# Maxima split and turned by one engine and sent straight to the query rows, operands laid out as they are loaded

## The chip, the core and the metric

The kernel runs on one core of a Trainium2 chip. The core has five engines, each with its own queue of instructions: TensorE (PE in the profile) multiplies matrices, VectorE (DVE) reduces and computes element by element, ScalarE (ACT) applies functions, GpSimd (POOL) computes element by element more slowly, and SyncE (SP) asks for transfers between memory (HBM) and on-chip memory. Engines run side by side and wait for each other through semaphores. TensorE writes into eight banks of an accumulation memory (PSUM); a bank may be written again when its reader is done. The metric is the time of one execution on the device in microseconds (us), lower is better, as the median of several runs.

## The reference

The input x is a sequence of 2048 tokens of width 512. The result mixes a 32-head attention (head width 16) and a gated feed-forward layer (inner width 1792), token by token:

```python
x = A_x
g = _sigmoid((x * gate_w).sum(-1, keepdims=True))
a = _A_ref(x, A_wqkv, A_wo)
b = _B_ref(x, B_w_gate, B_w_up, B_w_down)
return g * a + (1 - g) * b
```

```python
scores = jnp.einsum("bhqd,bhkd->bhqk", q, k) * scale
p = _softmax(scores, axis=-1)
o = jnp.einsum("bhqk,bhkd->bhqd", p, v)
...
g = jnp.einsum("bsd,df->bsf", x, w_gate)
u = jnp.einsum("bsd,df->bsf", x, w_up)
h = _sigmoid(g) * u
return jnp.einsum("bsf,fd->bsd", h, w_down)
```

## The kernel before

Everything is float32. For accuracy a product of two operands is made of three: each operand is split into a high part (rounded to a shorter format that TensorE takes) and a low part (the rest), and high x high, high x low and low x high are summed.

**Attention.** Heads go in 16 pairs. For a pair, `QS` and `KS` hold the query and key rows, one head in partitions 0 to 63 and one in 64 to 127. The softmax needs the largest score of each query. It is found first: a pass of matmuls (L282, in `sm_step`) makes scores of 128 queries by 512 keys, and VectorE reduces each to one column (L284). Sixteen such reductions complete a *part*: the maxima of 512 queries of one head, in a tile `stat` of 128 partitions by 4 blocks by 4. `turn_max` then turns a part: VectorE reduces the four columns of each query to one (L296, tile `msq`) and transposes it (L298, tile `mt`), so that queries lie along a row. The maxima, split in high and low, are written into two spare rows of `QS` (rows 48 and 49 of each half), where the second pass of matmuls (L577, in `st_part`), which takes 64 rows where the first took 48, subtracts them. ScalarE takes the exponential (L579), and TensorE multiplies with the values (L710, in `values`).

The way from `mt` to the rows of `QS` has two halves, and `turn_max` gives back a function for each. `send` splits on GpSimd (L98, L99, tile `mhl`) and writes 128 rows to memory at `m_d` (L302). `back` reads two rows from there into `QS` (L308), one transfer for the high and one for the low parts.

**Order.** The main loop has 256 periods (`for k in range(NPER)`), and each is written out by hand: `STEADY` holds two lists of words, and for each word the next matmul of a stream is put on TensorE's queue: `m0`, `m1` scores for maxima, `t0`, `t1` scores for the exponential, `d0`, `d1` half a matmul of other work (64 rows), so that two streams fill the two halves of TensorE. After each list come the 32 matmuls of the values. Seven banks go round between the streams by a table (`REUSE`). The `d` work is, first, query and key projections of later heads (`Sum`, L148), then the feed-forward layer (`Side`, L168), which is computed from mixtures of blocks of x and of the weights.

Work that is not on TensorE's list stands in a queue of closures, `later`. One is taken at the word `work`, three or four after each list, so these closures set the order of GpSimd and of the transfers that follow them on SyncE. After a list, `turn_max` is called for each full part; its `send` is put at the front of `later`, and its `back` is called two periods on. A part falls due every second period, from the two halves in turn. All transfers but two stand on SyncE's queue in the order in which the program was written, and each waits until the eighth transfer before it has landed.

**Mixtures.** `mixing` makes sums and differences of blocks of x on GpSimd, 16 pieces for each of two column pairs: `load` fetches up to four half tiles (L326), GpSimd adds and splits (L331, L347, L335), and the result goes to memory (L336), from where `mixed` reads it back (L356). `mixtures` does the same for weights: `raw` fetches tiles `r0` to `r5` (L376) as one or two half tiles each. `turn` puts a token on GpSimd's queue (L176) that a later matmul on TensorE waits for; it keeps the two halves from writing one bank at once.

Of the kernel before, what the change touches and what calls it, by code (L numbers as in the profile page):

```python
# [12 lines left out]
F32 = mybir.dt.float32  # L13
# [27 lines left out]
UPPER = FIRST + 4  # L41
EARLY = NPER - TAIL - 4
LOW, UP = 0, 1


@with_exitstack
def gated_mix(ctx, tc, x, xc, wqk, wv, wo, w_gu, w_down, gate_w, out):
    nc = tc.nc
    pe, act, dve, pool, sp = nc.tensor, nc.scalar, nc.vector, nc.gpsimd, nc.sync

# [25 lines left out]
    m_d = dram.tile([NPAIR, NC, 2, P, 2, 32], F32, name="m_d")  # L76

    warm = keep.tile([P, 1], F32, name="warm")
    dve.memset(warm, 0.0)
# [166 lines left out]
                    yield sp.dma_start((QS, KS)[t][p % 2][r:r + DH, cols].bitcast(F32), src[a, rows, cols])  # L246
# [22 lines left out]
    def sm_step(j):  # L269

        p, s = divmod(j, 32)
        qt, kh = divmod(s, 2)
        qs, ks = QS[p % 2], KS[p % 2]

        def one(b, i):
            part = (p, qt // 4, b)
            if part not in stat:
                stat[part] = keep.tile([P, 4, 4], F32, name=f"stat{p}_{qt // 4}_{b}", tag="stat", bufs=8)
                count[part] = 0
            r, g = 64 * b, 2 * kh + i  # L280
            t = bankm()
            pe.matmul(t, qs[r:r + KM, qt * P:(qt + 1) * P], ks[r:r + KM, g * 512:(g + 1) * 512],  # L282
                      start=True, stop=True)
            dve.tensor_reduce(stat[part][:, qt % 4, g:g + 1], t, axis=AX.X, op=ALU.max)  # L284
            count[part] += 1
            if count[part] == 16:
                full.append(part)
        return one
# [3 lines left out]
    def turn_max():  # L292
        part = full.pop(0)
        p, i, b = part
        m = square()
        dve.tensor_reduce(m[:, :4], stat.pop(part), axis=AX.X, op=ALU.max)  # L296
        mt = keep.tile([P, 32], F32, name=f"mt{p}_{i}_{b}", tag="mt", bufs=2)
        dve.transpose(mt, m)  # L298
        def send():
            hl = keep.tile([P, 2, 32], F32R, name=f"mhl{p}_{i}_{b}", tag="mhl", bufs=2)  # L300
            split(hl[:, 0, :], hl[:, 1, :], mt, pool, pool)
            sp.dma_start(m_d[p, i, b], hl.bitcast(F32))  # L302

        def back():
            rows = m_d[p, i, b].rearrange("(g t) a j -> a t g j", g=4)
            for a in range(2):
                r = 64 * b + 3 * DH + a
                sp.dma_start(QS[p % 2][r:r + 1, i * 512:(i + 1) * 512].bitcast(F32).rearrange(  # L308
                    "o (t g j) -> o t g j", g=4, j=32), rows[a, :4].unsqueeze(0))
        return send, back  # L310

    SIDES = (slice(0, 64), slice(64, 128))
    MIX = (((0, 0), "+", (1, 1)), ((0, 0), None, None)), (((0, 1), "-", (1, 1)), ((1, 0), "-", (0, 0))), (
        ((0, 0), "+", (0, 1)), ((1, 0), "+", (1, 1))), (((1, 1), None, None), ((1, 1), None, None))

    def mixing(pair):

        def load(j, b):
            e = keep.tile([P, 2, 512], F32R, name=f"xm{pair}_{j}_{b}", tag="ev", bufs=2)
            f = e.bitcast(F32)  # L320
            for g in (UP, LOW):
                first, sign, second = MIX[j][1 - g]
                for i, half in enumerate((first, second)):
                    if half:
                        r, c = half
                        sp.dma_start(f[SIDES[g], i, :], xc[2 * pair + c, 2 * r + b // 2, SIDES[b % 2], :])  # L326
# [12 lines left out]
        loaded = []  # L339
        later.append(lambda: loaded.append(load(*pieces[0])))  # L340
        for n, (j, b) in enumerate(pieces):
            yield
            signs = [MIX[j][1 - g][1] for g in (LOW, UP)]
            for rows, sign in zip([slice(0, P)] if signs[0] == signs[1] else SIDES, signs):
                if sign:
                    later.append(lambda n=n, r=rows, op=ALU.add if sign == "+" else ALU.subtract: add(loaded[n], r, op))
            later.append(lambda n=n: pool.tensor_copy(loaded[n][:, 1, :], loaded[n].bitcast(F32)[:, 0, :]))  # L347
# [18 lines left out]
    def mixtures():  # L366
        for cp in range(2):
            for fp in range(NF // 2):
                for a in range(2):
                    name = f"{cp}_{fp}_{a}"  # L370

                    def raw(n, *parts):
                        t = keep.tile([P, 512], F32, name=f"r{n}_{name}", tag="wr", bufs=4)
                        for (f, r), sides in parts:
                            for g in sides:
                                sp.dma_start(t[SIDES[g], :], w_gu[a, 2 * fp + f, r])  # L376
                        return t
# [9 lines left out]
                    x0 = raw(0, ((0, 0), [UP]), ((1, 0), [LOW]))  # L387
                    x1 = raw(1, ((1, 1), [UP, LOW]))
                    yield
                    w = ready(0, x0, x1, ALU.add)  # L390
                    r = raw(2, ((0, 0), [UP]), ((1, 1), [LOW]))
                    yield w
                    w = ready(1, r)
                    y = raw(3, ((1, 0), [UP]), ((0, 1), [LOW]))
# [3 lines left out]
                    z0 = raw(4, ((0, 0), [side]))  # L398
                    z1 = raw(5, ((0, 1), [side]))
# [184 lines left out]
    for t in range(2, NS, 2):  # L584
        two = [Sum(bankv(), tokens(t + a)) for a in range(2)]
        for g in (LOW, UP):
            first_max()
            for m in range(3 * KT):
                two[0].half(g)
                two[1].half(1 - g)  # L590
                if m == 5 or m == 8 and (g == LOW or t == 2):
                    first_max()
                if t == NS - 2 and (g, m) in ((LOW, 8), (UP, 2), (UP, 5), (UP, 8)):
                    next(ahead)
                while full:
                    for go in turn_max():
# [184 lines left out]
    outs, backs = [], []  # L781
    backlog = []
    for k in range(NPER):
        n = 2 * k
# [12 lines left out]
        else:  # L797
            group["t1"] = chain(st_part(k, 1), st_part(k + 1, 1))
        emit(STEADY[k % 2] if k < NPER - TAIL else LAST[k - NPER], **group)
        for go in backs:  # L800
            go()
# [138 lines left out]

def by_blocks(w):
    w = np.asarray(w)
    return w.reshape(2, 2, 2, 64, NF, P).transpose(4, 0, 3, 1, 2, 5).reshape(NF, 2, 64, 512)


# [20 lines left out]
```

## Time and profile before

| what | value |
|---|---|
| median of 3 runs | 1700.06 us (1697.31 to 1703.04) |
| the profiled execution | 1701.52 us, its span 1699.7 us, mean granted clock 0.996 |
| share of TensorE, VectorE, ScalarE, GpSimd that is busy | 99%, 85%, 79%, 60% |
| `xm<-in_xc_dram`, SyncE | 104 transfers, 128 KB each |
| `r<-in_w_gu_dram`, SyncE | 280 transfers, 128 KB each |
| `m_d<-mhl`, SyncE | 128 transfers, 32 KB each |
| `qs<-m_d`, SyncE | 256 transfers, 2 KB each |
| `pv_d<-sum`, SyncE | 64 transfers, 128 KB each |

A row of the profile names line, engine, operation and tiles (written<-read), with durations in us, or in ns where it says mean. An entry in brackets tells how long the engine stood idle before the row, and what ended it. "SPq" is SyncE's queue. A busy share is an average: what a change is worth is read at the places where TensorE stands still.

### The profile page before, as it was taken

Reading aid. Unit: us, or ns where it says so; the run is one execution under the profiler, and the core shown is the slowest. Engines: PE = TensorE matmul, PEld = TensorE weight load, DVE = VectorE, ACT = ScalarE, POOL = GpSimd, SP = SyncE. Lnnn points to the kernel's source line nnn. Section 1 sums busy time; section 2 is a strip of 40 time slices with the busy share of each in tenths; the row PEclk is TensorE's granted clock in tenths of the full one; section 3 lists DMA queues with packets and bytes.
Section 4 is the critical chain, followed back from the end, with each engine's and each line's share of the span. In section 5 each row is a group of like instructions: output and inputs, shape, how many; then the busy total and the mean of one; then the engine's idle time right before and its main releaser. Section 6 shows DMA issues by size and latency. Waiting matters only on the chain.

```text
span 1699.7 us, 43409 instructions
## 1 busy us (share of the span) xinstructions
PE 1684.2 (99%) x16552; PEld 1155.1 (68%) x16552; DVE 1441.1 (85%) x2450; ACT 1336.3 (79%) x2668; POOL 1026.5 (60%) x1193
## 2 busy tenths in 40 slices
PE   9999998999999999999999999999999999999999
PEld 7866665666666666666666566666666666578887
DVE  6899997999999999999998799999999999567543
ACT  4188886888888888888888799999999988973321
POOL 1146664358888787777664777777776765352110
PEclk9999999999999999999999999999999999999999
DMA  9625677364445454443347342424243423276752
GB/s 258 112 86 164 181 209 194 121 159 134 129 135 142 131 132 144 125 116 89 89 139 186 110 110 80 124 87 112 93 113 92 108 83 101 69 255 227 246 195 72
DMA packets 148944, 231.70 MB, mean 136 GB/s; under 512 B 40384, under 2 KB 57024, under 8 KB 145728
## 3 DMA queue, kind: packets, MB, share of 16 engines
q1 hardware_dynamic: 148448, 228.41, 47.4%
q8 instruction: 130, 2.13, 0.6%
q14 instruction: 78, 0.64, 0.1%
q10 hardware_dynamic: 288, 0.52, 0.1%
HBM read 148.90 MB, written 79.95 MB: 135 GB/s over the span
## 4 chain that ended last, share of the span: by engine, by line
PE 81%; DMA 1%; SPq 0%; ACT 0%; issue 0%; DVE 0%; POOL 0%; ACTq 0%
PE dn L168 23%; PE sm L710 18%; PE sm L282 8%; PE st L282 7%; PE sm L914 7%; PE st L710 6%; PE sm L577 4%; PE st L135 3%; PE st L577 2%; PE dn L914 2%; PE dn L148 2%; DMA m_d<-mhl 1%; DMA xm<-xm_d 0%; DMA xm<-in_xc_dram 0%; ACT p L579 0%; SPq L376 0%
## 5 line engine op out<-in xcount | busy, mean ns | idle before, releaser
L284 DVE TENSOR_REDUCE stat<-sm 128x1 f32<-128x512 f32 x1124 | 728.2, 682 | 66.4 <-PE st L577 26.8
L579 ACT ACTIVATE p<-sm 128x512 f32<-128x512 f32 x1217 | 686.8, 630 | 18.0 <-PE sm L577 15.7
L284 DVE TENSOR_REDUCE stat<-st 128x1 f32<-128x512 f32 x924 | 607.0, 683 | 62.7 <-PE st L282 24.6
L579 ACT ACTIVATE p<-st 128x512 f32<-128x512 f32 x831 | 499.4, 634 | 2.4 <-PE st L282 0.7
L168 PE MATMUL dn<-xm,mh 64*128 64x512 f32 x1568 | 486.4, 390 | 5.7 <-DMA xm<-xm_d 5.7
L577 PE MATMUL sm<-qs,ks 64*128 64x512 f32 x1217 | 447.0, 405 | 0.3 <-ACT p L579 0.2
L282 PE MATMUL sm<-ks,qs 48*128 48x512 f32 x1124 | 420.6, 422 | 0.3 <-ACT p L579 0.3
L282 PE MATMUL st<-ks,qs 48*128 48x512 f32 x924 | 369.1, 427 | 0.0
L710 PE MATMUL sm<-p,v 128*17 128x256 f32 x6080 | 366.2, 381 | 0.1
L577 PE MATMUL st<-qs,ks 64*128 64x512 f32 x831 | 325.6, 409 | 0.0
L168 PEld LDWEIGHTS dn<-xm,mh 64*128 64x128 f32 x1568 | 289.6, 185 | 35.2 <-DMA xm<-xm_d 7.3
L168 PE MATMUL dn<-xm,ml 64*128 64x512 f32 x784 | 304.8, 389 | 0.0
L728 POOL TENSOR_TENSOR sum<-sum,part 128x256 f32<-128x256 f32 x192 | 141.6, 737 | 256.5 <-ACT part L715 237.3
L710 PEld LDWEIGHTS sm<-p,v 128*17 128x17 f32 x6080 | 160.5, 97 | 170.6 <-ACT p L579 58.8
L282 PEld LDWEIGHTS sm<-ks,qs 48*128 48x128 f32 x1124 | 200.5, 185 | 85.9 <-DVE stat L284 57.6
L577 PEld LDWEIGHTS sm<-qs,ks 64*128 64x128 f32 x1217 | 219.3, 186 | 18.9 <-ACT p L579 3.3
L282 PEld LDWEIGHTS st<-ks,qs 48*128 48x128 f32 x924 | 167.7, 185 | 83.3 <-DVE stat L284 66.9
L410 POOL TENSOR_TENSOR m<-m,m 128x512 f32<-128x512 f32 x140 | 178.2, 1289 | 2.8 <-ACT m L512 2.5
L577 PEld LDWEIGHTS st<-qs,ks 64*128 64x128 f32 x831 | 152.7, 186 | 12.3 <-ACT p L579 1.5
L168 PEld LDWEIGHTS dn<-xm,ml 64*128 64x128 f32 x784 | 144.7, 185 | 11.9
L121 POOL TENSOR_TENSOR ml<-r,mh 128x512 fp32r<-128x512 f32 x112 | 144.0, 1286 | 7.7
L512 ACT ACTIVATE m<-dn 128x512 f32<-128x512 f32 x196 | 132.8, 677 | 0.0
(225 smaller groups left out, 2180.4 us busy)
## 6 DMA issues: line engine op xcount, KB each, us to landing
r<-in_w_gu_dram SPq DMA_DIRECT2D x280, 128.0 KB
gul<-gu_d SPq DMA_DIRECT2D x56, 512.0 KB
gu_d<-m SPq DMA_DIRECT2D x84, 256.0 KB
xm_d<-xm SPq DMA_DIRECT2D x32, 512.0 KB
xm<-xm_d SPq DMA_DIRECT2D x32, 512.0 KB
xm<-in_xc_dram SPq DMA_DIRECT2D x104, 128.0 KB
qs<-q_d SPq DMA_DIRECT2D x90, 128.0 KB
ks<-k_d SPq DMA_DIRECT2D x90, 128.0 KB
```

The lines of the kernel that those rows point to most:

```text
L121: pool.tensor_tensor(l, src, h.bitcast(F32), ALU.subtract)
L135: pe.matmul(o, a, b, start=(i == 0), stop=(i == len(ops) - 1))
L168: pe.matmul(self.o, a, b, start=(self.n == 0), stop=(self.n == len(self.ops) - 1))
L282: pe.matmul(t, qs[r:r + KM, qt * P:(qt + 1) * P], ks[r:r + KM, g * 512:(g + 1) * 512], start=True, stop=True)
L284: dve.tensor_reduce(stat[part][:, qt % 4, g:g + 1], t, axis=AX.X, op=ALU.max)
L410: pool.tensor_tensor(o, x, y, op)
L512: leave = lambda e, o: act.activation(e, o, AF.Copy)
L577: pe.matmul(o, ks[r:r + KR, (kt + a) * P:(kt + a + 1) * P], qs[r:r + KR, c * 512:(c + 1) * 512], start=True, stop=True)
L579: act.activation(pt[:, a, :], o, AF.Exp, scale=DH ** -0.5)
L710: pe.matmul(o[r:r + VW, :], v[:, 4 * k % 16 + a, h * VW:(h + 1) * VW], pts[b][:, a, 256 * i:256 * i + 256], start=(a == 0), stop=(a == 3))
L728: pool.tensor_tensor(s, s, e, ALU.add)
L914: pe.matmul(down[t], a, b, start=(f == 0 and m == 0), stop=(f == NF - 2 and m == 5))
```

## The change

Three things are changed.

1. `turn_max` splits before it transposes. VectorE reduces into `mx`, casts that to the high parts (L300 of the changed kernel), subtracts for the low parts (L301), with high and low of each block side by side in `msq`, and transposes four overlapping blocks of 32 columns at once (L305), so that high and low parts come out in neighbouring partitions. `send` is then four transfers from `mt` straight to the rows of `QS`, for four groups of 32 partitions. `back`, `m_d`, `mhl` and GpSimd's two instructions are gone. `stat` has 6 buffers in place of 8, `msq` one in place of two.
2. The host gives the blocks of x (`xmix`) and of the gate and up weights (`w_gu`) in the arrangement in which they are loaded, so that each piece of `xm` and each of `r0` to `r5` is one transfer.
3. The list of changes that came with it names token sums asked for by SyncE; in the diff no line of theirs is changed, but for what moves in line numbers.

```diff
-    square = ring(keep, 2, [P, 32], "msq")
-    for _ in range(2):
-        pool.memset(square(), 0.0)
+    square = turns([(keep.tile([P, 4], F32, name=f"mx{i}"), keep.tile([P, 40], F32R, name=f"msq{i}")) for i in range(1)])
+    for _ in range(1):
+        pool.memset(square()[1].bitcast(F32), 0.0)
...
-        m = square()
-        dve.tensor_reduce(m[:, :4], stat.pop(part), axis=AX.X, op=ALU.max)
-        mt = keep.tile([P, 32], F32, name=f"mt{p}_{i}_{b}", tag="mt", bufs=2)
-        dve.transpose(mt, m)
+        m, hl = square()
+        dve.tensor_reduce(m, stat.pop(part), axis=AX.X, op=ALU.max)
+        two = hl[:, :8].rearrange("p (t c) -> p t c", c=2)
+        dve.tensor_copy(two[:, :, 0], m)
+        dve.tensor_tensor(two[:, :, 1], m, two[:, :, 0].bitcast(F32), ALU.subtract)
+        f = hl.bitcast(F32)
+        blocks = bass.AP(f.tensor, f.offset, [f.ap[0], (2, 4), (1, 32)])
+        mt = keep.tile([P, 4, 32], F32, name=f"mt{p}_{i}_{b}", tag="mt", bufs=2)
+        dve.transpose(mt, blocks)
+
         def send():
-            hl = keep.tile([P, 2, 32], F32R, name=f"mhl{p}_{i}_{b}", tag="mhl", bufs=2)
-            split(hl[:, 0, :], hl[:, 1, :], mt, pool, pool)
-            sp.dma_start(m_d[p, i, b], hl.bitcast(F32))
-
-        def back():
-            rows = m_d[p, i, b].rearrange("(g t) a j -> a t g j", g=4)
-            for a in range(2):
-                r = 64 * b + 3 * DH + a
-                sp.dma_start(QS[p % 2][r:r + 1, i * 512:(i + 1) * 512].bitcast(F32).rearrange(
-                    "o (t g j) -> o t g j", g=4, j=32), rows[a, :4].unsqueeze(0))
-        return send, back
+            r = 64 * b + 3 * DH
+            rows = QS[p % 2][r:r + 2, i * 512:(i + 1) * 512].bitcast(F32).rearrange("a (t g j) -> a g t j", g=4, j=32)
+            for g in range(4):
+                sp.dma_start(rows[:, g], mt[32 * g:32 * g + 2])
+        return send
...
-            for g in (UP, LOW):
-                first, sign, second = MIX[j][1 - g]
-                for i, half in enumerate((first, second)):
-                    if half:
-                        r, c = half
-                        sp.dma_start(f[SIDES[g], i, :], xc[2 * pair + c, 2 * r + b // 2, SIDES[b % 2], :])
+            n = max(1 + (second is not None) for _, _, second in MIX[j])
+            sp.dma_start(f[:, :n, :], xmix[pair, j, b, :, :n, :])
...
-                    def raw(n, *parts):
+                    def raw(n, rows=slice(0, P)):
                         t = keep.tile([P, 512], F32, name=f"r{n}_{name}", tag="wr", bufs=4)
-                        for (f, r), sides in parts:
-                            for g in sides:
-                                sp.dma_start(t[SIDES[g], :], w_gu[a, 2 * fp + f, r])
+                        sp.dma_start(t[rows, :], w_gu[a, fp, n, rows, :])
                         return t
...
-        for go in backs:
-            go()
-        backs, outs, turned = outs, [], []
+        turned = []
         while full:
-            send, back = turn_max()
-            turned.append(send)
-            outs.append(back)
+            turned.append(turn_max())
```

How this moves instructions is shown at two places, with the buffers' numbers and the semaphores that each instruction waits for (DMAHW0 to DMAHW7 tell of transfers). First VectorE, where it turns a part of pair 8 in the main loop, before:

```order
L284 TENSOR_REDUCE stat8_0_0_10624<-sm0_69 128x1 [waits PE_49]
L296 TENSOR_REDUCE msq0_112<-stat8_0_1_10458 128x4 [waits DVE_49]
L298 STREAM_TRANSPOSE mt8_0_1_10743<-msq0_112 128x32 [waits DVE_49,Pool_49]
L284 TENSOR_REDUCE stat8_1_1_10772<-sm3_72 128x1 [waits PE_49]
L284 TENSOR_REDUCE stat8_0_0_10624<-st0_65 128x1 [waits PE_49]
```

and the same place of the changed kernel, whose lines are numbered otherwise (L286 is the reduction of scores):

```order
L286 TENSOR_REDUCE stat8_0_0_10508<-sm0_69 128x1 [waits PE_49]
L298 TENSOR_REDUCE mx0_111<-stat8_0_1_10342 128x4 [waits DVE_49]
L300 CAST msq0_112<-mx0_111 128x4 [waits DVE_49]
L301 TENSOR_TENSOR msq0_112<-mx0_111,msq0_112 128x4 [waits DVE_49]
L305 STREAM_TRANSPOSE mt8_0_1_10627<-msq0_112 128x128 [waits DMAHW2_49,DMAHW1_49,DMAHW7_49,DMAHW0_49,DVE_49]
L286 TENSOR_REDUCE stat8_1_1_10654<-sm3_72 128x1 [waits PE_49]
```

Two instructions come in between, each waits for the one ahead of it, and the transposition waits for the four transfers that read the tile's buffer two turns before, where it waited for GpSimd. Second SyncE, where the part `1_1` (pair 1, queries 512 to 1023) of one head is sent, before:

```order
L730 DMA pv_d_77<-sum0_3_1981 128x256 [waits DMAHW7_49,Pool_49]
L302 DMA m_d_79<-mhl1_1_0_2275 128x64 [waits DMAHW0_49,Pool_49]
L336 DMA xm_d_75<-xm0_1_2_2193 256x1x512 [waits DMAHW1_49,Pool_49]
L326 DMA xm0_1_3_2282<-in_xc_dram 64x512 [waits DMAHW2_49]
L326 DMA xm0_1_3_2282<-in_xc_dram 64x512 [waits DMAHW3_49]
L326 DMA xm0_1_3_2282<-in_xc_dram 64x512 [waits DMAHW4_49]
L326 DMA xm0_1_3_2282<-in_xc_dram 64x512 [waits DMAHW5_49]
L246 DMA qs0_103<-q_d_73 16x2048 [waits DMAHW6_49]
L246 DMA ks0_104<-k_d_74 16x2048 [waits DMAHW7_49]
L308 DMA qs1_105<-m_d_79 1x16x32 [waits DMAHW0_49]
L308 DMA qs1_105<-m_d_79 1x16x32 [waits DMAHW1_49]
```

and of the changed kernel:

```order
L722 DMA pv_d_77<-sum0_3_1967 128x256 [waits DMAHW1_49,Pool_49]
L311 DMA qs1_104<-mt1_1_0_2174 2x4x32 [waits DMAHW2_49,DVE_49]
L311 DMA qs1_104<-mt1_1_0_2174 2x4x32 [waits DMAHW3_49]
L311 DMA qs1_104<-mt1_1_0_2174 2x4x32 [waits DMAHW4_49]
L311 DMA qs1_104<-mt1_1_0_2174 2x4x32 [waits DMAHW5_49]
L331 DMA xm_d_75<-xm0_1_2_2179 256x1x512 [waits DMAHW6_49,Pool_49]
L321 DMA xm0_1_3_2265<-in_xmix_dram 128x1024 [waits DMAHW7_49]
L248 DMA qs0_102<-q_d_73 16x2048 [waits DMAHW0_49]
L248 DMA ks0_103<-k_d_74 16x2048 [waits DMAHW1_49]
```

The maxima go from `mt` to `QS` at the place where they went to memory; they wait for VectorE instead of GpSimd, and the two transfers that waited for the first to land are gone from the queue. The load of `xm` is one transfer. On TensorE and ScalarE the order is unchanged, and on GpSimd the two instructions of each split are left out.

More of the change, by code (lines that the diff above doesn't have):

```diff
@@ L43, with gated_mix @@
 LOW, UP = 0, 1
+MIX = ((((0, 0), "+", (1, 1)), ((0, 0), None, None)), (((0, 1), "-", (1, 1)), ((1, 0), "-", (0, 0))),
+       (((0, 0), "+", (0, 1)), ((1, 0), "+", (1, 1))), (((1, 1), None, None), ((1, 1), None, None)))
+BLOCKS = (((0, 0), (1, 0)), ((1, 1), (1, 1)), ((0, 0), (1, 1)), ((1, 0), (0, 1)), ((0, 0), (0, 0)), ((0, 1), (0, 1)))
 @with_exitstack
-def gated_mix(ctx, tc, x, xc, wqk, wv, wo, w_gu, w_down, gate_w, out):
+def gated_mix(ctx, tc, x, xc, xmix, wqk, wv, wo, w_gu, w_down, gate_w, out):
     nc = tc.nc
@@ L75, in gated_mix @@
     rec_d = dram.tile([P, 512], F32, name="rec_d")
-    m_d = dram.tile([NPAIR, NC, 2, P, 2, 32], F32, name="m_d")
     warm = keep.tile([P, 1], F32, name="warm")
@@ L277, in one @@
             if part not in stat:
-                stat[part] = keep.tile([P, 4, 4], F32, name=f"stat{p}_{qt // 4}_{b}", tag="stat", bufs=8)
+                stat[part] = keep.tile([P, 4, 4], F32, name=f"stat{p}_{qt // 4}_{b}", tag="stat", bufs=6)
                 count[part] = 0
@@ L397, in mixtures @@
                     side = LOW if a else UP
-                    z0 = raw(4, ((0, 0), [side]))
-                    z1 = raw(5, ((0, 1), [side]))
+                    z0 = raw(4, SIDES[side])
+                    z1 = raw(5, SIDES[side])
                     yield w
@@ L595, in gated_mix @@
                 while full:
-                    for go in turn_max():
-                        go()
+                    turn_max()()
             if g == LOW:
@@ L780, in gated_mix @@
     bank = bankm = place
-    outs, backs = [], []
     backlog = []
@@ L942, in by_blocks, with by_mixtures, rows @@
     w = np.asarray(w)
-    return w.reshape(2, 2, 2, 64, NF, P).transpose(4, 0, 3, 1, 2, 5).reshape(NF, 2, 64, 512)
+    w = w.reshape(2, 2, 2, 64, NF, P).transpose(4, 0, 3, 1, 2, 5).reshape(NF // 2, 2, 2, 64, 512)
+    return np.stack([np.concatenate([w[:, f, r] for f, r in (low, up)], axis=1) for up, low in BLOCKS], axis=1)
+def by_mixtures(xc):
+    def rows(pair, j, b, g, i):
+        half = MIX[j][1 - g][2 * i]
+        r, c = half or MIX[j][1 - g][0]
+        return xc[2 * pair + c, 2 * r + b // 2, 64 * (b % 2):64 * (b % 2) + 64]
+    return np.array([[[[[rows(pair, j, b, g, i) for i in range(2)] for g in (LOW, UP)] for b in range(4)]
+                      for j in range(4)] for pair in range(2)]).transpose(0, 1, 2, 3, 5, 4, 6).reshape(2, 4, 4, P, 2, 512)
 def kernel(A_x, A_wqkv, A_wo, B_x, B_w_gate, B_w_up, B_w_down, gate_w):
+    xc = np.asarray(A_x)[0].T.reshape(KT, P, NC, 512).transpose(2, 0, 1, 3)
     host = {
         "x": np.asarray(A_x)[0],
-        "xc": np.asarray(A_x)[0].T.reshape(KT, P, NC, 512).transpose(2, 0, 1, 3),
+        "xc": xc,
+        "xmix": by_mixtures(xc),
         "wqk": by_tiles(A_wqkv)[:8],
```

11 lines of the change are left out of this document (4 added, 7 removed).

## The prediction

> **What bounds the kernel now.** I read the page first: engine shares, then the chain of work that ended last.
>
> ```profile
> span 1699.7 us, 43409 instructions
> PE 1684.2 (99%) x16552; PEld 1155.1 (68%) x16552; DVE 1441.1 (85%) x2450; ACT 1336.3 (79%) x2668; POOL 1026.5 (60%) x1193
> PE 81%; DMA 1%; SPq 0%; ACT 0%; issue 0%; DVE 0%; POOL 0%; ACTq 0%
> ```
>
> TensorE sets the end almost alone. Nothing in the change takes a matmul away, so time can only come from where TensorE stands still, and be lost where something new makes it stand still. The next view is the busy time of each engine in stretches of 25 us; these are the columns PE, PEld, DVE, ACT, POOL, then the granted clock, the DMA share and GB/s. I looked for stretches where PE is under 25.00.
>
> ```profile
> 275.00:300.00 25.00, 20.68 (x190) 13.37 (x187) 16.62 (x29) 15.40 (x32) 8.50 (x13) 0.86 0.66 162
> ...
> 900.00:925.00 25.00, 24.58 (x272) 15.90 (x272) 22.55 (x41) 22.43 (x46) 16.49 (x19) 1.00 0.84 211
> 925.00:950.00 25.00, 19.75 (x196) 11.59 (x188) 15.81 (x28) 14.88 (x30) 13.54 (x15) 0.86 0.60 176
> ```
>
> Between the start and the tail there are two holes: 25.00 - 20.68 = 4.3 us near 280, and 5.25 + 0.42 = 5.7 us near 935. Both also lower the granted clock to 0.86, so each costs more than its idle time. The timeline of TensorE and the chain show how much more, and what was waited for.
>
> ```profile
> 283.27 0.79 PE L148 MATMUL dn<-xt,k2h 64*128 64x512 f32 x1 [4.32 <-POOLq L176]
> 283.16 0.61 POOL L347 CAST xm<-xm 128x512 fp32r<-128x512 f32 x1 [9.04 <-DMA xm<-in_xc_dram]
> 276.24 6.11 DMA xm<-in_xc_dram
> 284.06 0.43 PE dn L148
> 291.60 0.22 PE sm L282
> 918.55 9.75 DMA m_d<-mhl
> 932.88 7.04 DMA xm<-xm_d
> 942.04 2.93 PE sm L710 x32
> ```
>
> First hole: TensorE waits for GpSimd's token (L176), which stands in GpSimd's queue behind the cast L347, which waits for a load of `xm`. After it, matmuls go 0.43 apart instead of 0.22 to 0.23 until 288.75, some 13 steps, so 13 x 0.2 = 2.6 us more: **6.9 us**. Second hole: a late load of `xm` back from memory. Eight steps at the slow pace (8 x 0.2 = 1.6) and one block of the value product at 2.93 instead of 1.92 (the row below) make 5.7 + 1.6 + 1.0 = **8.3 us**. Together **15 us**. Why the loads were late is in SyncE's timeline and in its waits.
>
> ```profile
> 266.08 0.32 SPq L246 DMA_DIRECT2D qs<-q_d  x1
> 270.70 1.36 SPq L308 DMA_DIRECT2D qs<-m_d  x2
> ...
> 919.35 3.81 SPq L246 DMA_DIRECT2D ks<-k_d  x2
> 928.32 1.39 SPq L308 DMA_DIRECT2D qs<-m_d  x2
> ...
> SPq L308 <- DMA m_d<-mhl: 103.6, 54, 7.1
> ```
>
> Ahead of each late load SyncE stands at L308: from 266.40 to 270.70, 4.3 us, and from 923.16 to 928.32, 5.2 us, because the maxima's way out (`m_d<-mhl`) has to land before their way back may be asked for. Whatever is queued behind it on SyncE, the `xm` loads among it, waits too.
>
> **What goes.** (a) The trip through `m_d`, and with it every wait at L308. The load at 276.24 would have been asked for some 4.3 us sooner, and its last hole was 4.3 us. The second hole needs about its 5.7 idle us, and has 5.2 us from L308 at 928.32 and up to 7.1 us each from the ones before it. (b) Loads that were cut into half tiles become one issue each: `xm` from 104 issues to 32, `r` from 280 to 168. At 0.32 (266.08) to 0.68 (each of the two at 270.70) an issue, 184 fewer are 59 to 125 us of SyncE's time over the run. Of the bytes nearly all stay. (c) GpSimd loses two instructions a turn, 256 in all; it is busy 60% and nothing in the chain hangs on its speed, so I count them at nothing: what they leave is more of the 40% in which it idles already. (d) "SyncE asks for token sums" names nothing in this diff: the sums' stores stand on SyncE already (`pv_d<-sum SPq`), and still do. Nought. I take **-15 us** for both holes, bounds 0 and -15.
>
> **What comes.** VectorE now splits the maxima itself. A *turn* was a reduction (L296) and a transposition (L298); now it is reduction, cast, subtraction, transposition of four blocks, in a row, each waiting for the one ahead of it. VectorE's timeline shows two turns, which alternate:
>
> ```profile
> 621.13 0.68 DVE L284 TENSOR_REDUCE stat<-st 128x1 f32<-128x512 f32 x1
> 621.85 0.17 DVE L296 TENSOR_REDUCE msq<-stat 128x4 f32<-128x16 f32 x1
> 622.12 0.21 DVE L298 STREAM_TRANSPOSE mt<-msq 128x32 f32<-128x32 f32 x1
> 622.46 0.69 DVE L284 TENSOR_REDUCE stat<-st 128x1 f32<-128x512 f32 x1
> ...
> 623.66 1.28 DVE L284 TENSOR_REDUCE stat<-st 128x1 f32<-128x512 f32 x2
> ...
> 632.76 0.16 DVE L296 TENSOR_REDUCE msq<-stat 128x4 f32<-128x16 f32 x1
> 633.03 0.21 DVE L298 STREAM_TRANSPOSE mt<-msq 128x32 f32<-128x32 f32 x1
> 633.49 0.69 DVE L284 TENSOR_REDUCE stat<-sm 128x1 f32<-128x512 f32 x1 [0.25 <-PE st L577]
> ```
>
> No row shows a cast or subtraction of 4 columns. The nearest are these, for small instructions; the third gives the slope.
>
> ```profile
> L79 DVE MEMSET warm<- 128x1 f32 x1 | 0.1, 59 | 0.8 <-PEq L955 0.8
> L843 DVE TENSOR_SCALAR g<-g 128x16 f32<-128x16 f32 x1 | 0.2, 175 | 0.0
> L284 DVE TENSOR_REDUCE stat<-sm 128x1 f32<-128x512 f32 x1124 | 728.2, 682 | 66.4 <-PE st L577 26.8
> ```
>
> So each new instruction lasts between 0.06 and 0.175; it reads and computes as L843 and L296 do, so I take 0.16. From reduction to reduction of 16 and 512 columns, (0.68 - 0.16) / 496 is 1.05 ns a column, so 96 more columns in the transposition cost 0.10 (bounds: 0, and 3 x 0.21 if each block costs a transposition). Gaps between dependent instructions: 0.04 at 621.81 to 621.85, 0.10 at 622.02 to 622.12, where one more wait (for GpSimd) stands between. I take two new gaps of 0.04 and leave the last one as it was, less 0.04, since its waits for four DMAs stand ahead of the wait for VectorE and can be passed while the subtraction runs. The turn grows by 2 x 0.16 + 2 x 0.04 - 0.04 + 0.10 = **0.46 us** (bounds 0.15 and 0.75).
>
> What covers it? Three things. VectorE idles after a turn: 622.33 to 622.46, and 633.24 to 633.49, 0.13 and 0.25. Back-to-back reductions start 0.60 apart though one lasts 0.68 (1.28 for two), so another 0.08. And the matmuls that need the banks have a little slack:
>
> ```profile
> 624.99 0.29 PEld L282 LDWEIGHTS st<-ks,qs 48*128 48x128 f32 x2 [0.20 <-DVE stat L284]
> 624.84 0.40 PE L282 MATMUL sm<-ks,qs 48*128 48x512 f32 x1
> 625.08 0.51 PE L282 MATMUL st<-ks,qs 48*128 48x512 f32 x2
> 620.07 1.92 PE L710 MATMUL st<-p,v 128*17 128x256 f32 x32
> ```
>
> The weight load at 624.99 waited for the reductions that ended at 623.66 + 1.28 = 624.94; its matmul started at 625.08, on TensorE's own pace of 0.24 after 624.84. A later release by 0.09 is free, more is not. The eight reductions of the period after a turn stand nearly end to end, so a late turn reaches this last matmul in full. That gives thresholds of 0.13 + 0.08 + 0.09 = **0.30** and 0.25 + 0.08 + 0.09 = **0.42**; beyond them TensorE stands still at each turn. With 0.46 the cost is 0.16 and 0.04. The next view, of the tile `mt`, counts the turns: 128, of which the first four come before 88 us.
>
> ```profile
> L298 DVE STREAM_TRANSPOSE mt<-msq x128: 211/211/214, 60.9 to 1468.5; 128x32 f32<-128x32 f32 x128
> ```
>
> So 62 x 0.16 + 62 x 0.04 = 12.4 us, and about 1 us for the two pairs at the start, where reductions are packed as tightly: **+13 us** (bounds: 0, and 62 x (0.45 + 0.33) = 48).
>
> [...]
>
> On SyncE a turn now asks for four small DMAs in place of three. They stand where the first stood, two pieces of a pair's maxima are due 22 us later, and at the same 0.32 to 0.68 four issues are 1.3 to 2.7 us in place of 1.36 and the store's own: nothing, while 59 us or more go elsewhere.
>
> **The sum.** Against the profiled execution, 1701.5 us (span 1699.7): 1701.5 - 15 + 13 = 1699.5, against a median of the three runs of 1700.06 (1697.3 to 1703.0); I say **1699**. A measurement tells 0.3%, 5.1 us, from no change.
>
> **Rivals.** *VectorE's longer turn is covered* (1686 to 1692): the growth is under 0.30 to 0.36, the holes go. [...] Against it: L296 and L843. Chance 0.22. *VectorE sets the pace* (slower): at a growth of 0.60 the turns cost 62 x (0.30 + 0.18) = 30 us, 1701.5 - 15 + 30 = 1717; from a growth of 0.52 on it outweighs the holes by over 5 us. For it: five waits ahead of one transposition, and four blocks that could cost more than their columns. Against it: the slope. Chance 0.24. *The holes stay*, or half of them: DMAs are busy 0.84 of the stretch from 900, and four small DMAs a turn may land behind the same large ones; then VectorE's transposition, which waits for the DMAs of two turns before, may even wait itself, though it has 22 us and the longest landing shown is 9.75. 1701.5 + 13 - 7 = 1707, 1714 if none goes. For it: the DMA share; against it: DMA share 0.66 and 0.60 in the stretches of the holes themselves, so the queue was not full but asked too late. Chance 0.14. *Forecast*: holes gone, turns at 0.16 and 0.04, 1694 to 1705. Chance 0.40.
>
> **Range and chances.** Low end: the covered case in full, 1686. High end: a growth of 0.60 with the holes gone, 1717, which holds the staying holes too. Faster by over 0.3% (under 1695) is the covered case and a third of the forecast: 0.36. Within 0.3%: over half of the forecast and parts of the rivals' near ends: 0.35. Slower (over 1705): most of VectorE's rival and of the staying holes: 0.29.
>
> **What will show it.** The holes: PE back at 25.00 in both stretches, and no wait of SyncE for maxima. The turn: the reduction after a turn starts 0.61 (622.46 - 621.85) or 0.73 (633.49 - 632.76) after the turn's first instruction now; I expect about 0.9 for both, and the last matmuls of the period behind a turn 0.16 or 0.04 late. If the cast or the subtraction shows under 0.10, the covered case is right; if the transposition shows over 0.45, VectorE's. If TensorE waits for `xm` again, the holes were the DMAs' and not L308's.

## The result, and the profile after

| kernel | runs | median us | lowest to highest |
|---|---|---|---|
| before | 4 | 1698.68 | 1694.77 to 1703.04 |
| changed | 4 | 1718.98 | 1717.76 to 1719.17 |

The changed kernel takes 1.0117 times as long, 95% interval 1.0091 to 1.0144: slower by 20 us, where 1699 was forecast, and 2 us above the range. The page of the profiled execution (span and instructions, engine shares, the chain that ended last):

```profile
span 1717.1 us, 43465 instructions
PE 1702.4 (99%) x16552; PEld 1129.9 (66%) x16552; DVE 1498.5 (87%) x2706; ACT 1338.0 (78%) x2668; POOL 974.4 (57%) x936
PE 92%; DVE 6%; DMA 1%; ACT 0%; POOL 0%; issue 0%; SPq 0%; POOLq 0%; ACTq 0%
```

VectorE, which was 0% of the chain, is 6% of it now. Busy time by stretches of 25 us, in the columns of the prediction (PE, PEld, DVE, ACT, POOL, granted clock, DMA share, GB/s), shows where it is not:

```profile
275.00:300.00 25.00, 24.50 (x267) 15.42 (x270) 23.61 (x44) 19.28 (x40) 10.89 (x12) 1.00 0.47 134
900.00:925.00 25.00, 25.00 (x267) 16.00 (x266) 23.69 (x46) 22.25 (x47) 14.73 (x15) 1.00 0.81 213
925.00:950.00 25.00, 25.00 (x280) 16.00 (x274) 23.22 (x45) 21.78 (x45) 17.13 (x17) 1.00 0.61 180
1450.00:1475.00 25.00, 23.75 (x182) 14.18 (x174) 20.87 (x38) 18.28 (x39) 9.53 (x10) 0.86 0.18 62
```

The holes near 280 and 935 us are gone, with the clock back at 1.00, as forecast; the half microsecond that is still missing from the first stretch is of the kind that is shown below. A new one stands near 1460. The other sign that was named, no wait of SyncE for maxima, did not come: SyncE stands at `send` (L311) 122 times, for VectorE now (total us, times, longest us).

```profile
SPq L311 <- DVE stat L286: 214.5, 122, 7.9
```

The next view is that of the tile `msq`: the least, middle and greatest duration in ns of each instruction on it, and when they start.

```profile
L300 DVE CAST msq<-mx x128: 169/170/819, 61.6 to 1481.6; 128x4 fp32r<-128x4 f32 x128
L301 DVE TENSOR_TENSOR msq<-mx,msq x128: 162/164/1308, 61.8 to 1481.8; 128x4 fp32r<-128x4 f32 x128
L305 DVE STREAM_TRANSPOSE mt<-msq x128: 311/311/315, 62.0 to 1482.0; 128x128 f32<-128x128 f32 x128
```

The middle values are those of the forecast: 0.17, 0.16, 0.31. The greatest are not: one and the same cast of four columns takes 0.17 or 0.82 us, one and the same subtraction 0.16 or 1.31. In the trace 31 casts and 17 subtractions, in 42 of the 128 turns, last over 40 ns longer than the middle value, by 6.4 and 16.0 us in all. What else goes on then is in the timeline, of which VectorE's and GpSimd's rows are shown (start, duration, engine, line; lines of the changed kernel: L239 and L236 split a projection, L326 mixes):

```profile
108.33 0.61 POOL L239 CAST qh<-qk 128x512 fp32r<-128x512 f32 x1 [3.74 <-ACT qk L505]
108.63 0.17 DVE L298 TENSOR_REDUCE mx<-stat 128x4 f32<-128x16 f32 x1
...
108.83 0.17 DVE L300 CAST msq<-mx 128x4 fp32r<-128x4 f32 x1
...
109.02 1.30 POOL L236 TENSOR_TENSOR qk<-qk,qh 128x512 fp32r<-128x512 f32 x1
109.04 1.30 DVE L301 TENSOR_TENSOR msq<-mx,msq 128x4 fp32r<-128x4 f32 x1
...
110.37 0.31 DVE L305 STREAM_TRANSPOSE mt<-msq 128x128 f32<-128x128 f32 x1
110.40 1.27 POOL L326 TENSOR_TENSOR xm<-xm 64x512 f32<-64x512 f32 x1
```

GpSimd starts its subtraction at 109.02. VectorE's starts at 109.04, ends when GpSimd's has ended, and does four columns' work in the time of GpSimd's 512. Over the whole trace each of the 48 long instructions ends 19 to 33 ns after an instruction of GpSimd has ended, and no short one began while GpSimd was executing an instruction that outlasted it. TensorE's timeline has the price (the blocks of the value product begin the periods, which are 5.52 apart in both kernels otherwise):

```profile
106.85 1.92 PE L702 MATMUL sm<-p,v 128*17 128x256 f32 x32
...
111.31 0.49 PE L570 MATMUL st<-qs,ks 64*128 64x512 f32 x1 [0.48 <-DVE stat L286]
...
113.54 0.84 PE L702 MATMUL sm<-p,v 128*17 128x256 f32 x11
```

113.54 - 106.85 = 6.69, 1.17 more than 5.52. Between 97 and 364 us 11 periods are longer by that. The hole near 1460 is a turn in which both instructions lasted long, 0.82 and 1.21 us, while GpSimd ran two instructions of 2.52 us together:

```profile
1455.60 2.52 POOL L403 TENSOR_TENSOR m<-m,m 128x512 f32<-128x512 f32 x2 [2.45 <-ACT m L505]
...
1456.09 0.82 DVE L300 CAST msq<-mx 128x4 fp32r<-128x4 f32 x1
...
1456.94 1.21 DVE L301 TENSOR_TENSOR msq<-mx,msq 128x4 fp32r<-128x4 f32 x1
```

**The account**, profile against profile. What periods last beyond 5.517 us, their *extras*, sums to 16.3 before (15.1 of it the two holes) and to 27.6 after (18 periods of over 0.9 us: 22.3; 17 of 0.1 to 0.9: 3.8; the rest 1.5). The last four periods, 9.6 longer together in both kernels, are left out. Of the 18, 17 have a turn with a held subtraction; the other stands behind the hole near 1460, where its block of values takes 3.61 in place of 1.92. The first block of values starts at 90.3, not 88.4, 1.9 later (the *start*), and from the last one to the end (the *tail*) it takes 204.8, not 200.6, 4.2 more. 1699.7 - 15.1 + (27.6 - 1.2) + 1.9 + 4.2 = 1717.1.

The theory from here on: VectorE's cast and subtraction wait for the instruction that GpSimd is executing. The rivals: A, the new layouts of the loads cost the time; B, the layouts alone took the holes away; C, the longer chain of dependent instructions costs it, whatever GpSimd does.

### The profile page after: what moved, and what is told of

Its sections match the earlier page's. It is cut to its first block, busy times and chain, and to the rows that moved or that the text cites. A ratio compares the mean times of both kernels' runs of the same rounds, so it can differ in the third digit from the quotient of the medians.

```text
span 1717.1 us, 43465 instructions
## 1 busy us (share of the span) xinstructions
PE 1702.4 (99%) x16552; PEld 1129.9 (66%) x16552; DVE 1498.5 (87%) x2706; ACT 1338.0 (78%) x2668; POOL 974.4 (57%) x936
## 4 chain that ended last, share of the span: by engine, by line
PE 92%; DVE 6%; DMA 1%; ACT 0%; POOL 0%; issue 0%; SPq 0%; POOLq 0%; ACTq 0%
PE dn L170 26%; PE sm L702 20%; PE sm L284 8%; PE st L284 7%; PE sm L901 7%; PE st L702 6%; PE dn L150 4%; DVE stat L286 4%; PE st L137 4%; PE sm L570 3%; PE st L570 2%; PE dn L901 2%; PE st L150 2%; DVE msq L301 1%; DVE mt L305 0%; PE st L84 0%
## 5 line engine op out<-in xcount | busy, mean ns | idle before, releaser
L286 DVE TENSOR_REDUCE stat<-sm 128x1 f32<-128x512 f32 x1124 | 723.2, 677 | 44.2 <-PE st L570 18.7
L286 DVE TENSOR_REDUCE stat<-st 128x1 f32<-128x512 f32 x924 | 602.2, 676 | 33.6 <-PE sm L570 16.6
L570 PE MATMUL sm<-qs,ks 64*128 64x512 f32 x1217 | 456.2, 411 | 3.8 <-DVE stat L286 3.5
L570 PE MATMUL st<-qs,ks 64*128 64x512 f32 x831 | 331.8, 415 | 5.4 <-DVE stat L286 5.4
L170 PE MATMUL dn<-xm,ml 64*128 64x512 f32 x784 | 308.8, 394 | 0.0
```

The lines of the kernel that those rows point to most:

```text
L170: pe.matmul(self.o, a, b, start=(self.n == 0), stop=(self.n == len(self.ops) - 1))
L570: pe.matmul(o, ks[r:r + KR, (kt + a) * P:(kt + a + 1) * P], qs[r:r + KR, c * 512:(c + 1) * 512], start=True, stop=True)
```

## The experiments

Diffs are against the changed kernel, where nothing else is said.

**1 and 2: the two halves of the change apart.** The first puts back `turn_max`, `m_d`, `send` and `back` of before; the second puts back the loads of before (`xc` in half tiles, `w_gu` by blocks) and keeps the new turn.

```diff
-        return send
+        return send, back
...
-            turned.append(turn_max())
+            send, back = turn_max()
+            turned.append(send)
+            outs.append(back)
```

> The changed kernel with the turn of before put back (split by GpSimd, store to m_d, wait at L308, load from there); the new layouts of the loads stay. Theory (VectorE's cast and subtraction wait for whatever GpSimd is executing): no cast or subtraction on VectorE in the main loop, so no turn over 0.8 us, no extra period from turns; the two holes near 280 and 935 us come from SyncE standing at L308, so they are still there, whole or in part: 1692 to 1702. Rival A (the new layouts of the loads cost the time): 1713 to 1720, though VectorE is as before. Rival B (the layouts alone took the holes away): 1684 to 1689.

```diff
-            sp.dma_start(f[:, :n, :], xmix[pair, j, b, :, :n, :])
+                        sp.dma_start(f[SIDES[g], i, :], xc[2 * pair + c, 2 * r + b // 2, SIDES[b % 2], :])
...
-                        sp.dma_start(t[rows, :], w_gu[a, fp, n, rows, :])
+                                sp.dma_start(t[SIDES[g], :], w_gu[a, 2 * fp + f, r])
```

> The changed kernel with the loads of before (half tiles, 184 more issues on SyncE); the new turn stays. Theory: long casts (over 0.25 us) and long subtractions as in the changed kernel, some 40 of 128 turns, and the holes stay away since nothing waits for maxima on SyncE: 1712 to 1722. Rival A (the layouts cost the time): 1684 to 1700. Rival B (the layouts alone took the holes away): the two holes are back on top of the long turns, 1727 to 1735.

Old turn: 1695.63, ratio to before 0.9982 (0.9965 to 1.0). Old loads: 1718.50, ratio 1.0112 (1.0084 to 1.014). So the whole loss comes with the turn; rival A is out. Busy time by stretches, old turn first, then old loads:

```profile
275.00:300.00 25.00, 25.00 (x276) 16.45 (x276) 23.11 (x42) 21.39 (x44) 12.81 (x20) 1.00 0.47 140
925.00:950.00 25.00, 21.27 (x204) 13.19 (x202) 17.93 (x32) 17.74 (x37) 18.00 (x22) 0.93 0.46 138
```

```profile
275.00:300.00 25.00, 24.51 (x270) 15.57 (x272) 23.62 (x44) 19.07 (x39) 10.76 (x12) 1.00 0.61 182
925.00:950.00 25.00, 25.00 (x284) 15.79 (x274) 23.21 (x45) 21.79 (x46) 17.12 (x17) 1.00 0.69 191
```

The second hole stays with the old turn (3.7 us of TensorE's time) and goes with the new one, whatever the loads, so rival B is out for it. The chain of the run with the old turn shows the way: the store to `m_d` takes 8.4 us to land, until 919.1, then SyncE issues the loads that wait for it and, behind them, a load of `xm` (8.7 us), for which TensorE waits until 930.9. That SyncE waits for maxima is not enough for a hole: in the changed kernel it waits for them too, and neither hole is there. The first is gone in both, so this pair does not say whose it was; a second profile of the kernel before (below) has 0.9 us of it where the first had 4.3, and that of run 11, which has the old turn and the old loads too, has 3.3.

**3: as many instructions, of another kind.**

```diff
-        dve.tensor_copy(two[:, :, 0], m)
-        dve.tensor_tensor(two[:, :, 1], m, two[:, :, 0].bitcast(F32), ALU.subtract)
+        dve.tensor_reduce(two[:, :, 0].bitcast(F32), m.unsqueeze(2), axis=AX.X, op=ALU.max)
+        dve.tensor_reduce(two[:, :, 0].bitcast(F32), two[:, :, 0:1].bitcast(F32), axis=AX.X, op=ALU.max)
```

> The changed kernel with cast and subtraction each replaced by a reduction of 4 columns over one element: as many dependent instructions on VectorE and the same transposition, but none that reads two operands or copies. The low half of the maxima is left at zero. Theory: both stay at 0.16 to 0.20 us each time, no turn over 1.0 us, the periods of over 0.9 us extra fall away, some 22 us of TensorE: 1688 to 1697. Rival C (the longer dependent chain costs the time, whoever else is running): 1713 to 1720.

1696.14, ratio to before 0.9973 (0.9958 to 0.9988): 22.8 us less than the changed kernel, with the chain as long. The tile `msq`:

```profile
L300 DVE TENSOR_REDUCE msq<-mx x128: 157/158/164, 61.1 to 1456.3; 128x4 f32<-128x4 f32 x128
L301 DVE TENSOR_REDUCE msq<-msq x128: 157/157/161, 61.3 to 1456.5; 128x4 f32<-128x4 f32 x128
```

Of the 256, 58 began while GpSimd executed an instruction that outlasted them, and none lasted over 164 ns. Rival C is out. No period is longer by over 0.9 us; all extras together are 2.8.

**4: no split.** Reduction, transposition of 32 columns, and the row of maxima sent as it is. (A maximum that is rounded is still the same number above and below the softmax's fraction line.)

```diff
+        dve.tensor_reduce(m[:, :4], stat.pop(part), axis=AX.X, op=ALU.max)
+        dve.transpose(mt, m.bitcast(F32))
...
+                sp.dma_start(row[:, g], mt[32 * g:32 * g + 4])
```

> The changed kernel without any split: reduction, transposition of 32 columns as before, and four DMAs that send the one row of maxima straight to the query rows; the low half is left at zero. Theory: turns as short as before, holes away, no m_d: 1683 to 1690, faster than both kernels. Rival C (chain length) gives the same here; rival A (layouts) says 1710 or more.

1691.25, ratio 0.9959 (0.9946 to 0.9973). The main loop is at its pace: extras of 0.4 us in all. It is over the expected 1690 since start and tail are as long as in the changed kernel, which no theory so far explains.

**5: the kernel before, profiled again**, for the tail.

> The kernel before, profiled once more. The four profiles taken since have a tail (from the last product with the values on) of 204.4 to 204.9 us, the profile of before one of 200.6 us. If the tail belongs to the kernels, it is 200 to 201 us here again; if it belongs to the execution that was profiled, it is 204 to 205 us. Holes near 280 and 935 us of any size, 1692 to 1705 us in all.

1695.88 (one run), tail 200.6: the tail belongs to the kernels. Its holes cost 9.3 us in place of 15.1; their size changes from run to run, and the kernel before spreads over 12.5 us in 25 runs, where one row, without holes, spreads over 1.3 in 10.

**6 and 7: one of the two subtractions gone**, GpSimd's in the first, VectorE's in the second.

```diff
-            pool.tensor_tensor(e, e.bitcast(F32), h.bitcast(F32), ALU.subtract)
```

> The changed kernel, VectorE's program untouched, with one GpSimd instruction taken away: the subtraction (1.30 us, 128x512) that makes the low halves of the later queries and keys, so that their low halves hold the whole value. Theory (VectorE's subtraction waits for what GpSimd is executing): the 11 periods of +1.17 us between 97 and 364 us lose their long subtraction, 10 to 13 us less than the changed kernel: 1705 to 1710. Rival C (chain length) and any rival in which GpSimd plays no part: 1716 to 1720.

```diff
-        dve.tensor_tensor(two[:, :, 1], m, two[:, :, 0].bitcast(F32), ALU.subtract)
```

> The changed kernel without VectorE's subtraction; the low half of the maxima is left at zero. The cast stays and so do its waits, 31 with 6.4 us in all, of which TensorE feels what is over the turn's cover. Theory: the 16 us of waits of the subtraction go, and what a GpSimd instruction that starts during the cast held up goes with them; long turns are left only where the cast itself is held: 1696 to 1704. Rival (the cast alone would be held as long as both together): 1712 to 1720.

Without GpSimd's: 1714.86, only 4 us less, between the two ranges that were expected; **a miss**. VectorE's and GpSimd's rows of the timeline, in the turn shown above, which should have become short:

```profile
108.07 0.61 POOL L238 CAST qh<-qk 128x512 fp32r<-128x512 f32 x1 [3.74 <-ACT qk L504]
...
108.76 1.29 POOL L325 TENSOR_TENSOR xm<-xm 64x512 f32<-64x512 f32 x1
108.77 1.30 DVE L300 TENSOR_TENSOR msq<-mx,msq 128x4 fp32r<-128x4 f32 x1
```

GpSimd's next instruction (L325, the mixing of x) has moved up into the place of the one taken away, and holds VectorE as long. What holds it is whatever GpSimd executes there, not L236: in the changed kernel's trace, the holders are casts, subtractions and sums of seven lines. Without VectorE's subtraction: 1694.62 (0.9971, 0.9961 to 0.9982), a little under what was expected. The cast's own waits (to 819 ns still) are mostly inside what a turn is covered for.

**8 and 12: the start moved by nanoseconds, then by 0.19 us.** In the first the cast is made by a reduction, in the second there are two.

```diff
-        dve.tensor_copy(two[:, :, 0], m)
+        dve.tensor_reduce(two[:, :, 0], m.unsqueeze(2), axis=AX.X, op=ALU.max)
+        dve.tensor_reduce(two[:, :, 0], two[:, :, 0:1].bitcast(F32), axis=AX.X, op=ALU.max)
```

(The second `+` line stands in run 12 alone.)

> The changed kernel with the cast made by a reduction over one element, which takes and gives the same numbers; the subtraction stays. Theory: the reduction never lasts over 0.2 us, and the subtraction meets GpSimd's instruction itself, so that the wait of the two together is about what it was (22 us): 1712 to 1720. Rival (only what copies or casts is held, and the subtraction's length comes from the cast ahead of it): 1692 to 1700.

1698.96, ratio 0.9994 (0.9985 to 1.0004): **a miss**, inside the rival's range, and the most telling one. The rival's reason is out all the same: eight subtractions are long here with no cast ahead of them. Two turns in this run's timeline, rows of VectorE and GpSimd:

```profile
108.64 0.16 DVE L300 TENSOR_REDUCE msq<-mx 128x4 fp32r<-128x4 f32 x1
...
108.83 1.33 POOL L236 TENSOR_TENSOR qk<-qk,qh 128x512 fp32r<-128x512 f32 x1
108.83 0.16 DVE L301 TENSOR_TENSOR msq<-mx,msq 128x4 fp32r<-128x4 f32 x1
...
130.93 1.30 POOL L236 TENSOR_TENSOR qk<-qk,qh 128x512 fp32r<-128x512 f32 x1
130.94 1.31 DVE L301 TENSOR_TENSOR msq<-mx,msq 128x4 fp32r<-128x4 f32 x1
```

The reduction is 12 ns shorter than the cast, so the subtraction starts at +0.396 us of the turn in place of +0.408. In the first turn GpSimd's subtraction starts 3 ns ahead of it: VectorE is not held, and GpSimd's lasts 1.33 in place of 1.30. In the second GpSimd is 7 ns ahead, and VectorE is held for 1.14 us. Eight subtractions are held in this run in place of 17. In the 11 turns in which the two subtractions start within 10 ns, GpSimd is 2 to 4 ns ahead nine times, and VectorE is not held; twice it is 5 and 7 ns ahead, and VectorE is. In the changed kernel GpSimd was 13 to 17 ns ahead in all 11 turns of that kind. So the waits depend on who comes first, and in the changed kernel that was decided by some ten nanoseconds in turn after turn. If that is so, coming clearly later must be worse than either:

> The changed kernel with the cast made by a reduction over one element and a second such reduction behind it, so that the subtraction starts some 0.19 us later than with one. Where one reduction stood, the subtraction started at +0.396 us of the turn and GpSimd's 1.30 us subtraction at +0.393 to +0.509, and VectorE mostly had its way. Theory (whoever starts first keeps the other out): at about +0.59 every turn between 97 and 364 us, 24 of them, finds GpSimd's subtraction running and lasts 1.1 us longer: 1708 to 1725. Rival (GpSimd's instruction plays no part, only the chain's length): 0.03 us a turn more, 1699 to 1703.

1736.91, ratio 1.0233 (1.0215 to 1.0252): 38 us more for an instruction of 0.16 us, beyond the expected 1725, in the theory's direction. All 24 turns from 99 to 381 us are held, whichever of the two kinds: the subtraction lasts 1.12 to 1.30 us in each, and each costs TensorE 1.16 to 1.18. Rows of VectorE and GpSimd in the timeline of one of them:

```profile
111.86 1.29 POOL L236 TENSOR_TENSOR qk<-qk,qh 128x512 fp32r<-128x512 f32 x1
111.86 0.16 DVE L301 TENSOR_REDUCE msq<-msq 128x4 fp32r<-128x4 f32 x1
...
112.05 1.12 DVE L302 TENSOR_TENSOR msq<-mx,msq 128x4 fp32r<-128x4 f32 x1
```

The reduction at 111.86, beside the same GpSimd instruction, is untouched; the subtraction behind it waits. Behind 400 us, where the subtraction is mostly short, the longer chain costs 0.09 and 0.22 us a turn by the two kinds. The expectation had counted 0.03 there.

**9 to 11: the tail.** Nothing in the tail's code differs, but `stat` has a ring of 6 in place of 8 buffers, and every tile behind it lies elsewhere.

```diff
-                stat[part] = keep.tile([P, 4, 4], F32, name=f"stat{p}_{qt // 4}_{b}", tag="stat", bufs=6)
+                stat[part] = keep.tile([P, 4, 4], F32, name=f"stat{p}_{qt // 4}_{b}", tag="stat", bufs=4)
```

(This is run 9. In run 10 the same number goes from 6 to 8, on the kernel of experiment 4; in run 11 from 8 to 6, on the kernel before.)

> The changed kernel with a ring of four score tiles in place of six (128 bytes less in each partition; VectorE writes and reads them in turn, so no wait comes of it), which moves the operands that lie behind the ring: the tail's moving operand then lies a multiple of 256 bytes from its weights, as in the kernel before, not 128 bytes off. Theory (the tail's 4 us come from where the operands lie in SBUF): tail of 200.6 us instead of 204.8, the median at 1714 to 1716. Rival (the tail's pace comes from the new loads or the new turn): 204.8 us and 1718 to 1720.

> The kernel that sends one row of maxima without a split, with the ring of eight score tiles that the kernel before had, which puts the tail's operands back at the distance of before. Theory of the places: tail of 200.6 us, 1686 to 1688 in all. Rival: 204.8 us, 1690 to 1692.

> The kernel before with a ring of six score tiles in place of eight and nothing else: 128 bytes less in each partition. Theory of the places: a tail of 204.4 to 204.8 us instead of 200.6, the median 1702 to 1704. Rival: 200.6 us and 1698 to 1700.

The group of the tail's largest product (count, busy us, mean ns of one), a fence each for the kernel before, for the same with a ring of 6, for one row with 6 and with 8, and for the changed kernel with 6 and with 4:

```profile
L914 PE MATMUL sm<-wd_h,hl 128*128 128x512 f32 x192 | 62.7, 389 | 0.0
```

```profile
L914 PE MATMUL sm<-wd_h,hl 128*128 128x512 f32 x192 | 63.9, 395 | 0.0
```

```profile
L896 PE MATMUL sm<-wd_h,hl 128*128 128x512 f32 x192 | 63.9, 395 | 0.0
```

```profile
L896 PE MATMUL sm<-wd_h,hl 128*128 128x512 f32 x192 | 62.7, 389 | 0.0
```

```profile
L901 PE MATMUL sm<-wd_h,hl 128*128 128x512 f32 x192 | 63.8, 394 | 0.0
```

```profile
L901 PE MATMUL sm<-wd_h,hl 128*128 128x512 f32 x192 | 63.0, 391 | 0.0
```

The last 858 matmuls, all of 512 columns, follow each other within 194.4 us in the first and fourth, 198.2 in the second and third, 198.3 and 195.7 in the last two. The kernel before with a ring of 6 has a median of 1704.96, ratio 1.0042 (1.0027 to 1.0058), 6.7 us more, of which the tail, 204.4, has 3.8; the rest is not explained. One row with a ring of 8: **1686.98, ratio to before 0.9939 (0.9921 to 0.9957)**, the fastest of all, its tail 201.0, with the start back at 88.2 from 89.9 as well. The changed kernel with 4: 1715.38, inside the expected range, but with a tail of 202.2, 2.6 us less in place of 4.2. So the places do it. Taken product by product, what run 9's expectation put up (a multiple of 256 bytes between the two operands) holds in run 9 too. By the addresses in the built programs, the products of `wd_h` and `wd_l` with `hl` lie a multiple of 256 bytes apart there and start 227 ns apart (median); those of `weights` with `hl`, `oh` and `ol` do not, and start 229 to 231 apart, which leaves the tail half way. In all 14 profiles, groups of over 60 such matmuls have medians of 226.5 to 227 ns where the distance is such a multiple, and of 229 to 234 where it leaves 64, 128, 320, 384 or 448 bytes when divided by 512. How slow each distance is stays without an explanation.

## Why the prediction was wrong, point by point

- **The holes, -15.** Right: both gone, 15.1 in the profile. For the second the reason is shown as far as the old turn, whose chain runs through `m_d` and the wait at L308. The first is absent with either half of the change and of changing size in the kernel before; its cause stays open. In a second profile both holes together cost 9.3, so that 15 was the upper part of what could be had.
- **"So each new instruction lasts between 0.06 and 0.175; ... I take 0.16."** This is the step that failed. The middle values bear it out (0.17 and 0.16), and so does the growth of a turn by 0.46 (0.44 where nothing is held; the reduction behind it starts 0.84 or 0.85 after the turn's first instruction, where about 0.9 was expected). But the rows that it was read from could not show a wait for GpSimd: L296 is a reduction, of the kind that is never held in experiment 3, and L843 began while GpSimd executed nothing. Of the 256 new instructions 48 last longer, up to 0.82 and 1.31 us, because GpSimd is executing something. The upper bound should have been GpSimd's own rows for a subtraction of 512 columns, 1.29 us (L234 of the kernel before).
- **"Nothing in the chain hangs on its speed, so I count them at nothing."** The same error from GpSimd's side. In the kernel before that was true: of VectorE's 2237 instructions in the main loop 2219 were reductions, which were never held in experiment 3, and transpositions, which took 211 to 214 ns in all 128 turns. The change made VectorE's turn wait for GpSimd without a semaphore, so that no view of waits shows it: it shows only as a long instruction, of up to 0.82 and 1.31 us where the middle values are 0.17 and 0.16.
- **+13 for the turns.** Measured: 26.4 net of what stood there before, of which 22.3 are the 18 long periods. Without them the turns would have been cheaper than forecast: experiment 3, with a chain as long, has 2.8 in all. The thresholds of 0.30 and 0.42 were too low: a growth of 0.62 in experiment 12 costs 0.22 and 0.09, so the cover is about 0.40 and 0.53.
- **The rivals.** "VectorE sets the pace" named the right engine and side, and 1717 was near; its mechanism (waits ahead of the transposition, a dear transposition) was wrong: the transposition took 0.31, as estimated.
- **Start and tail, 0.** The prediction had no term for the ring of `stat`, 6 buffers in place of 8, though that moves every tile behind it. Tail +4.2, start +1.9 in the profiled executions; with the ring alone turned from 6 to 8, experiment 10 got back 3.8 in the tail and 1.7 at the start. The tail is borne out by run 11, the start is not: 88.9 with a ring of 6, between the 88.4 and 89.1 of the two profiles of the kernel before.

The runs show who waits for whom: casts and subtractions held to within 33 ns of GpSimd's end, 256 reductions never, and GpSimd keeping VectorE out from 5 ns ahead on, though not at 2 to 4 by the profile's start times. What in the chip makes them wait is not shown. With that much known, the bound stands in the trace of before: GpSimd was 60% busy, in instructions of up to 1.33 us in the main loop. The price does not: it hung on the order of starts in each turn.

## What to carry to other kernels

Before giving VectorE a cast or a two-operand instruction (the two kinds that were held here) on a path that TensorE waits for, see what GpSimd executes at that point of the order: as far as these runs go, the new instruction's duration is bounded by GpSimd's longest there, not by its own size (1.31 us for four columns beside GpSimd's 1.30 for 512). Where a tiny instruction has a middle of 0.16 us and a greatest of 1.3, lay both engines' timelines side by side; taking away the one GpSimd instruction found there need not help, since the next moves up (4 us less in experiment 6), while writing the cast as a reduction over one element did (20 us less in experiment 8). And when a change alters the size or the number of buffers, compare the pace of matmuls in stretches that it does not touch (here 194.4 and 198.3 us for the same 858).

## What the runs showed of the hardware that was not expected

- That VectorE is kept out shows in no wait, only in length: 1.31 us for four columns, ended 19 to 33 ns after GpSimd's instruction. It was decided alike turn after turn (in the changed kernel GpSimd came 13 to 17 ns ahead in all 11 turns of one kind), so that a reduction in the cast's place, 12 ns shorter and never held itself, was worth 20 us (experiment 8), and 0.19 us more cost 38 (experiment 12).
- The pace of a matmul of 512 columns went with where its operands lie in SBUF: on average 227 ns from start to start in one placement and 231 in another (194.4 and 198.2 us for the last 858), repeated within 0.2 us in every profile of the same placement, with a granted clock of 1.00 in both. In the large groups, products whose operands lie a multiple of 256 bytes apart kept 227 in each placement (medians), and the others took 229 to 234.
